# Batch numerators of a sketched attention: three batches as quads of 288 columns, and a new issue order

## Chip, cores and metric

One core of one Trainium2 chip. The metric is the device time of one execution in microseconds (us). A few hardware words: PE is TensorE (matmuls), DVE is VectorE, ACT is ScalarE, POOL is GpSimd, SP is SyncE, which here only issues DMAs. PSUM is the memory that PE writes; here it is eight banks of 512 float32 columns.

## The reference

An attention with degree-two sketch features, and then a mixing block over its output:

```python
def phi(x):                                   # 32 -> 64 features
    a = einsum('rd,bhsd->bhsr', S1, x)        # r = 8
    b = einsum('rd,bhsd->bhsr', S2, x)
    return einsum('bhsi,bhsj->bhsij', a, b).reshape(..., r * r)
q_p, k_p = phi(q), phi(k)
kv  = einsum('bhsf,bhsd->bhfd', k_p, v)
num = einsum('bhsf,bhfd->bhsd', q_p, kv)
den = einsum('bhsf,bhf->bhs', q_p, k_p.sum(2)) + 1e-06
x = (num / den) laid out as (B, S, H * D)

theta = x @ w_theta
zr, zi = x * cos(theta), x * sin(theta)
y = w_tok_r @ zr + w_tok_i @ zi               # over the 1088 tokens
u = x + y
out = u + relu(u @ w_ch)
```

There are 4 batches, 4 heads, 1088 tokens and a head dimension of 32, so x is 4 x 1088 x 128. The two token weights are 1088 x 1088.

## The kernel before

The tokens of a batch are 9 chunks of 128 (the last one holds 64). Three chunks make a group, so a batch has three groups of 384 columns. The kernel doesn't issue its work as it is written. Every step is first recorded by `op(engine, ..., function, writes, reads)`, each with a number; `vop` is the same for DVE. Then `run` takes the numbers in the order of a list written out by hand, `ORDER`, and `issue` calls the functions in that order. Each engine's own stream is the part of the list that belongs to it, executed in order; semaphores make a step wait for what it reads and for its buffers. A second list, `STARTS`, has a planned start for each step. `run` gives each buffer the slot of its class that has been free longest by these planned times, and `issue` puts short filler products (`spin`) on PE into planned gaps. Classes are sets of equal slots: `big` (22 of 1152 float32 columns), `zs` (5 of 2176), `g3` (5 of 768), `g1` (6 of 384), `ps` (the eight PSUM banks).

The stages of a batch are these.

- Keys: the features of k and their products with v (`kv`, 64 x 32 for each head). For batches 2 and 3, which are named in `QUADS`, kv is turned by two transposes and multiplied with a block mask into two halves of 32 features (`kvbd` of 256 columns). For 0 and 1 it is one transpose and 128 columns.
- Queries: `query_slices` turns q, and `levels` forms the two sketch factors in PSUM by products with q as weights (`exact`, `whole`). ACT copies them to `lv`, and a run of DVE steps ("den") scales one factor by the reciprocal of the denominator.
- Numerators, `outputs_x`. For each group DVE forms the outer products of the factors, 768 columns (`outer`). In batches 0 and 1 PE turns them (six transposes of 128 a group, line 1131), ACT copies them to SBUF (line 1135), two products on tiles of 128 x 64 give a group of x (`num`), and ACT copies that to `xT` (line 1144). In batches 2 and 3 DVE turns the features in 32 x 32 blocks (`V.transpose`, line 1109), and 32 products of 96 columns on the sixteen 32 x 32 tiles of PE (`quads`) give the group in four banks, which ACT copies by four copies of 96 columns (line 1121).
- Batches 1 to 3 (`XTURN`) also need x with tokens on the partitions. DVE turns the whole of `xT`, SP stores it to DRAM and fetches it back in another order.
- Angles: for each group, `theta` is a product on PE, ACT and DVE reduce the angle, ACT takes the two sines (lines 1203 and 1205), and DVE multiplies x with them into `z`.
- Token weights: 17 rows of 1088 KB come as 64-bit words, each into a `zs` slot. ACT (lines 643 and 645) and DVE decode a row into a `big` slot, in halves.
- Mixing: batches 0 and 1 are multiplied row by row (`mix_row`; "mix0_0" is all three groups of batch 0, 17 rows). Batches 2 and 3 are taken together by seven products of a Strassen-Winograd scheme (`winograd`), with additions on DVE and POOL.
- Outputs: `finish` multiplies with w_ch, adds on DVE, turns the result in 32 x 32 blocks and stores it. The last part of batch 3's first half (160 columns) goes by `finish_turned`, which transposes on PE instead.

Step 3 of the list is a dummy Sin of one column on ACT (line 433), issued before ACT's other work. Step 1 is 39 fillers on PE at the start.

Of the kernel before, what the change touches and what calls it, by code (L numbers as in the profile page):

```python
# [22 lines left out]
P = 128  # L23
# [115 lines left out]
)  # L139
WARM = 0  # L140
FILL = 5.0
LOAD_LEAD = 60.0
RAW_LEAD = 30.0
CHAINS = ((0,), (1,), (2, 3))
# [35 lines left out]
class Layout:  # L180
# [67 lines left out]
    def run(self):  # L248
        slots = {c: [[0.0, None] for _ in range(n)] for c, (n, _) in self.classes.items()}
        for b in self.bufs:  # L250
            b.left = len(b.ops)
# [52 lines left out]
def act(n):  # L304
    return 0.17 + 0.00083 * n
# [1238 lines left out]
```

## Time and profile before

| what | value |
|---|---|
| runs, us | 217.79, 218.53, 217.53 (median 217.79) |
| span of the profiled execution, us | 215.9 |
| median of the runs less that span, us | 1.9 |
| granted TensorE clock | 0.995 |
| busy PE / DVE / ACT / POOL, us | 208.9 / 174.3 / 114.5 / 59.7 |
| HBM read / written, MB | 29.84 / 4.00 |

The profile has one execution. Its span runs from the first to the last instruction; 1.9 us is what the median of the runs has beyond it, and stands in for the launch around the span. A group's line gives the code line, the engine, the operation, what it writes and reads with partitions x elements, the count, the busy time and the mean duration in ns. Nearly all PE products have the line 399, that of a helper, so they are told apart by buffer names and shapes. In the timeline a row is the start, the length and what ran. Products on PE are pipelined, so the distance between starts is their cost, not the length of one.

### The profile page before, as it was taken

What the parts mean: (1) busy time and instruction counts of PE and PEld (TensorE: products, weight loads), DVE (VectorE), ACT (ScalarE), POOL (GpSimd) and SP (SyncE); (2) the same over time, 40 slices, a digit from 0 to 9 for tenths busy, and PEclk for the clock granted to TensorE, in tenths of its full rate; (3) what the DMA queues carried; (4) which work ended last, traced back from release to release, by engine and by line L of the source; (5) the groups of instructions that cost most, each with busy time, mean ns of one, the idle gap of its engine ahead of it and who ended that gap; (6) DMA issues with size and microseconds to landing.
All of it is one profiled execution on the core that took longest, in us unless ns stands there. A gap on an engine that the chain in (4) does not pass through costs nothing.

```text
span 215.9 us, 5832 instructions
## 1 busy us (share of the span) xinstructions
PE 208.9 (97%) x2396; PEld 152.8 (71%) x2396; DVE 174.3 (81%) x343; ACT 114.5 (53%) x256; POOL 59.7 (28%) x105
## 2 busy tenths in 40 slices
PE   7899999999999999999999999999999999999992
PEld 7677798868866666866668666667677776666781
DVE  1799998999999998999999798885994747456263
ACT  4899989999998895798704233363810000000000
POOL 1272740306400000604004100000006489950403
PEclk9999999999999999999999999999999999999998
DMA  6999999995998993192002402424050420010735
GB/s 222 395 418 419 384 365 420 425 315 97 360 285 267 416 432 145 75 308 45 0 0 32 74 3 112 114 109 112 2 88 15 67 39 0 0 23 8 125 55 103
DMA packets 28046, 37.09 MB, mean 172 GB/s; under 512 B 20564, under 2 KB 23044, under 8 KB 25844
## 3 DMA queue, kind: packets, MB, share of 16 engines
q1 hardware_dynamic: 22868, 31.86, 42.4%
q0 software_dynamic: 1552, 3.25, 7.2%
q10 hardware_dynamic: 3600, 1.62, 2.8%
q8 instruction: 19, 0.31, 0.6%
q14 instruction: 7, 0.06, 0.1%
HBM read 29.84 MB, written 4.00 MB: 157 GB/s over the span
## 4 chain that ended last, share of the span: by engine, by line
PE 63%; DMA 18%; ACT 14%; issue 2%; SPq 1%; DVE 1%; POOL 1%; POOLq 0%; ACTq 0%
PE ps L399 61%; DMA zs<-w_tok 13%; DMA big<-k_l 5%; ACT big L645 4%; ACT big L643 3%; ACT lv L1056 1%; PE ps L1131 1%; ACT big L1021 1%; ACT g L1199 1%; ACT g L1202 1%; ACT g L1205 1%; ACT g L1203 1%; POOL out L1299 1%; SPq L671 0%; ACT g L1135 0%
## 5 line engine op out<-in xcount | busy, mean ns | idle before, releaser
L399 PE MATMUL ps<-big,zs 128*128 128x384 f32 (+2 forms) x380 | 110.5, 436 | 0.0
L399 PEld LDWEIGHTS ps<-big,zs 128*128 128x128 f32 x380 | 66.9, 190 | 32.5
L379 POOL TENSOR_TENSOR big<-big,big 128x544 f32<-128x544 f32 x16 | 22.1, 1458 | 48.6 <-DVE big L379 44.6
L399 PE MATMUL ps<-big,big 128*32 128x32 f32 (+2 forms) x352 | 22.8, 234 | 0.0
L643 ACT ACTIVATE big<-zs 128x1088 f32<-128x1088 f32 x17 | 20.9, 1231 | 1.5 <-DMA zs<-w_tok 0.9
L379 DVE CUSTOM_DVE_ANT_0 big<-big,big 128x2176 uint16<-128x2176 uint16 x17 | 21.5, 1275 | 0.0
L645 ACT ACTIVATE big<-zs 128x1088 int32<-128x1088 uint32 (+1 forms) x18 | 21.4, 1194 | 0.3 <-DMA zs<-w_tok 0.3
L1338 ACT COPY big<-ps 80x256 f32<-80x256 f32 x1 | 0.4, 368 | 39.6 <-DMA out<-g 39.6
L399 PEld LDWEIGHTS ps<-big,big 128*32 128x32 f32 (+1 forms) x352 | 15.3, 124 | 6.8 <-issue 0.8
L1276 ACT COPY g<-ps 128x384 f32<-128x384 f32 (+1 forms) x6 | 2.5, 466 | 23.4 <-PE ps L399 23.4
L379 DVE TENSOR_TENSOR big<-big 128x544 f32<-128x544 f32 x8 | 9.5, 1204 | 5.6 <-PE ps L399 5.6
L383 DVE TENSOR_SCALAR big<-big 128x1088 int32<-128x1088 int32 x17 | 12.2, 719 | 0.0
L379 POOL TENSOR_TENSOR mf<-mv,sm 128x32 f32<-128x32 f16 (+1 forms) x3 | 0.8, 262 | 39.1 <-DVE sm L379 39.1
L428 PE MATMUL ps<-idle 128*128 128x112 bf16 (+1 forms) x67 | 10.0, 312 | 1.3 <-POOL idle L430 1.3
L379 DVE TENSOR_TENSOR g<-lv 128x768 f32<-128x768 f32 x12 | 11.1, 950 | 0.1
L399 PEld LDWEIGHTS ps<-w,big 128*128 128x128 f32 (+1 forms) x76 | 9.8, 189 | 1.4
L379 DVE TENSOR_TENSOR big<-big,hf 128x1152 f32<-128x1152 f32 x8 | 10.7, 1351 | 0.0
L399 PE MATMUL ps<-w,big 128*128 128x128 f32 (+1 forms) x76 | 10.5, 278 | 0.0
L399 PE MATMUL ps<-sbk,g 128*128 128x64 f32 x72 | 10.0, 276 | 0.3 <-ACT g L793 0.3
L379 DVE TENSOR_TENSOR zs<-zs,g 128x384 f32<-128x384 f32 (+2 forms) x24 | 9.8, 447 | 0.2
L386 DVE SCALAR_TENSOR_TENSOR big<-ps,even,big 128x384 f32<-128x384 f32 (+1 forms) x10 | 4.8, 493 | 6.3 <-PE ps L399 6.2
L1199 ACT ACTIVATE g<-ps 128x384 f32<-128x384 f32 x12 | 5.9, 504 | 7.3 <-PE ps L399 7.3
(199 smaller groups left out, 379.2 us busy)
## 6 DMA issues: line engine op xcount, KB each, us to landing
zs<-w_tok SPq DMA_DIRECT2D x17, 1088.0 KB, 10.6
big<-k_l SPq DMA_DIRECT2D x5, 576.0 KB, 13.2
big<-v_l SPq DMA_DIRECT2D x4, 576.0 KB, 15.6
big<-q_l SPq DMA_DIRECT2D x3, 576.0 KB, 10.7
big<-hf POOLq DMA_DIRECT2D x3, 576.0 KB, 10.0
far<-zs SPq DMA_DIRECT2D x3, 576.0 KB, 2.8
zs<-far SPq DMA_DIRECT2D x12, 144.0 KB, 4.3
big<-k_l ACTq DMA_DIRECT2D x2, 576.0 KB, 4.4
```

The costliest lines, as they stand in the source:

```text
L379: eng.tensor_tensor(out=o, in0=a, in1=b, op=f)
L383: (eng or V).tensor_scalar(out=o, in0=a, scalar1=s1, scalar2=s2, op0=op0, **kw)
L386: (eng or V).scalar_tensor_tensor(out=o, in0=a, scalar=s, in1=b, op0=op0, op1=op1)
L399: T.matmul(o, lhs, rhs, start=start, stop=stop, skip_group_check=True)
L428: T.matmul(nowhere()[:, :n], idle()[:, 0:P], idle()[:, :n], start=True, stop=True, skip_group_check=True)
L643: op("A", 0.22 + n * 0.0009, lambda: A.activation(dfn(), words_of(raw(), n)[1].bitcast(F32), AF.Prelu, scale=2.0**-112, alpha=-(2.0**32)), ...
L645: op("A", 0.22 + n * 0.0009, lambda: A.activation(stp(), words_of(raw(), n)[0].bitcast(U32), AF.Copy, scale=2.0**-29), [stp], [raw])
L1021: op("A", act(GW) + 0.1, lambda g=g, tr=tr: A.activation(f()[:, g * GW:(g + 1) * GW], tr(), AF.Copy, scale=s()[:, 0:1]), [(f, g)], [tr, (s ...
L1056: op("A", act(480), lambda g=g, lp=lp: A.copy(lv().rearrange("p l (c n) -> p l c n", n=HR)[:, :, g * GC:(g + 1) * GC], lp().rearrange("p c ...
L1131: T.transpose(tr()[:, i * P:(i + 1) * P], qp()[:, i * H + 2 * n:i * H + 2 * n + 2].rearrange("p h i j -> p (h i j)"), ident())
L1199: op("A", act(GW), lambda cs=cs, th=th: A.activation(cs()[:, 0], th(), AF.Copy, bias=ROUND), [(cs, 0)], [th])
L1276: op("A", act(w), lambda: A.copy(u(), yp()[:, :w]), [uT], [yp])
```

## The change

- `QUADS` holds batch 1 too: its features are turned by DVE, its kv is prepared in two halves, and the transposes on PE and their copies are gone for it.
- In batches 1, 2 and 3 the three groups of turned features go to one buffer of 2304 columns, and there are 32 products of 288 columns for the whole batch in place of 32 of 96 for each group; four ACT copies of 288 columns follow. The buffer is of class `zs`, whose slots grow from 2176 to 2304 columns; `g3` has 4 slots for 5.
- In `levels`, `whole` takes only the 64 valid columns of the last chunk as weights.
- `finish_turned` is four recorded steps (transposes, copy, products, addition) with a buffer of its own for the result.
- The order is another one throughout. `STARTS` is gone: the slots are listed (`SLOTS`), and the fillers too (`GAPS`; 25 in all). Of the order itself: the dummy Sin comes behind the decoding of most rows; steps of batch 1's denominator come ahead of batch 0's first z, its outer products ahead of the last; SP issues rows 9 to 16 behind batch 1's way through DRAM; batch 3's last turn of 384 columns (step 908, with its stores) is the list's last step.

```diff
--- before
+++ after
 ORDER = (
-    29, 32, 4, 2, 5, 0, 1, 3, 34, 30, 356, 50, 33, 102, 44, 96, 6, 108, 103, 36, 7, 51, 366, 54, 144, 8, 97, 10, 9,
...
-    982, 925, 1000, 984, 983, 1008, 1001, 936, 1009, 1002, 1003, 937, 1004, 1005, 1010, 1006, 932, 1012, 1011, 933,
-    1013, 1007, 934, 938, 1014, 935, 1015, 939, 1016, 1017, 1018, 940, 1019, 941, 942, 943,
+    0, 4, 32, 1, 5, 29, 2, 33, 30, 144, 44, 139, 120, 108, 121, 143, 145, 6, 7, 109, 50, 146, 10, 140, 141, 126, 8, 9,
...
+    893, 894, 901, 902, 903, 986, 987, 818, 904, 980, 981, 989, 982, 954, 990, 895, 906, 905, 907, 909, 988, 955, 819,
+    983, 910, 911, 912, 913, 984, 914, 908,
 )
-STARTS = (
...
+GAPS = {51: 5, 11: 1, 79: 3, 90: 3, 92: 4, 436: 2, 168: 1, 117: 3, 119: 3}
+SLOTS = (
...
 WARM = 0
-FILL = 5.0
 LOAD_LEAD = 60.0
 RAW_LEAD = 30.0
 CHAINS = ((0,), (1,), (2, 3))
@@ -146,7 +98,7 @@
 KEEP = (2, 3)
 KEEP_CLS = "big"
 PAIR = (2, 3)
-QUADS = (2, 3)
+QUADS = (1, 2, 3)
 QTURN = (3,)
 XTURN = (1, 2, 3)
 PARTS = ((0, 384), (384, 544))
@@ -155,7 +107,7 @@
 RDMA = (False,) * 4
 QDMA = (False, False, False, False)
 UDMA = (True, True, False, False)
-TILE16, TILE32, TILE64, QUAD = 0.045, 0.12, 0.15, 0.65
+TILE16, TILE32, TILE64, QUAD = 0.045, 0.12, 0.15, 1.25
 ADD_FLY = 9.0
 ADD_FLY2 = 3.1
 QFIX = 2.006
@@ -246,33 +198,14 @@
         return o
 
     def run(self):
-        slots = {c: [[0.0, None] for _ in range(n)] for c, (n, _) in self.classes.items()}
-        for b in self.bufs:
-            b.left = len(b.ops)
         self.order = [self.ops[i] for i in ORDER]
-        for o, at in zip(self.order, STARTS):
-            o.start = at / 100.0
-            o.end = o.start + o.dur + o.fly
-            for b in o.bufs:
-                if b.slot is None and b.cls is not None:
-                    free = [(s[0], i) for i, s in enumerate(slots[b.cls]) if s[1] is None]
-                    b.slot = min(free)[1]
-                    slots[b.cls][b.slot][1] = b
-            for b in o.bufs:
-                b.left -= 1
-                b.end = max(b.end, o.end)
-                if not b.left and b.slot is not None:
-                    slots[b.cls][b.slot] = [b.end, None]
-
-    def issue(self, pools, fill, span):
-
-        last, on = 0.0, False
+        for b, slot in zip([b for b in self.bufs if b.cls is not None], SLOTS):
+            b.slot = slot
+
+    def issue(self, pools, fill):
         for o in self.order:
-            if o.eng == "P":
-                if on:
-                    for _ in range(int((o.start - last - 0.08) * FILL)):
-                        fill()
-                last, on = o.end, on and o is not span[1] or o is span[0]
+            for _ in range(GAPS.get(o.i, 0)):
+                fill()
             for b in o.bufs:
                 if b.ap is None:
                     b.ap = view(pools[b.cls](b.slot), b.shape, b.dt)
@@ -343,10 +276,10 @@
 
     classes = {
         "big": (22, 1152),
-        "zs": (5, 2176),
+        "zs": (5, 2304),
         "lv": (1, 5 * NT),
         "hf": (6, 576),
-        "g3": (5, 768),
+        "g3": (4, 768),
         "g1": (6, 384),
         "sm": (13, 192),
         "ps": (8, 512),
@@ -428,7 +361,7 @@
         T.matmul(nowhere()[:, :n], idle()[:, 0:P], idle()[:, :n], start=True, stop=True, skip_group_check=True)
 
     op("G", 0.3, lambda: G.memset(idle(), 0.0), [idle], [], due=-20.0)
-    first = op("P", 3.2, lambda: [spin(112) for _ in range(39)], [nowhere], [idle], due=-10.0)
+    op("P", 3.2, lambda: [spin(112) for _ in range(39)], [nowhere], [idle], due=-10.0)
     op("V", 1.25, constants, [hm, bdm, halfpi, ones], [])
     op("A", 1.5, lambda: A.activation(warm(), halfpi(), AF.Sin), [warm], [halfpi], due=0.0)
 
@@ -1048,8 +981,10 @@
 
             def whole(g=g, o=o):
                 for i in range(GC):
-                    x = f()[:, (g * GC + i) * P:(g * GC + i + 1) * P]
-                    mm(o(i)[:, 2 * HR:], x, mf[b]().rearrange("p t h r -> p (t h r)"), False, i == GC - 1)
+                    c = g * GC + i
+                    n = min(P, S - c * P)
+                    x = f()[:, c * P:c * P + n]
+                    mm(o(i)[:n, 2 * HR:], x, mf[b]().rearrange("p t h r -> p (t h r)"), False, i == GC - 1)
 
             op("P", 0.4, exact, [lp], [h, mv[b]], hold=[lv])
             op("P", 0.7, whole, [lp], [f, mf[b]])
@@ -1089,6 +1024,7 @@
         xt = xT[b] = buf("big", (NC * P,), F32, "xT")
         z = zt[b] = buf("zs", (NK, DM), F32, "z")
         bd = kvb[b]
+        qt = buf("zs", (NC, H, 2, SQ), F32, "qt") if b in QUADS else None
         for g in range(NG):
             at("num", b, "_", g)
             qp = buf("g3", (CH, R, R), F32, "qp")
@@ -1104,23 +1040,9 @@
             else:
                 vop(CH * R * R, lambda f=outer: f(V, 0, 1), [qp], [lv], lk=1)
             if b in QUADS:
-                qt = buf("g3", (GC, H, 2, SQ), F32, "qt")
-                xq = [buf("ps", (GC, SQ), F32, "xq") for _ in range(NQ)]
-                vop(CH * R * R, lambda qt=qt, qp=qp: V.transpose(out=qt().rearrange("p c h f t -> p (c h f t)"),
-                                                                 in_=qp().rearrange("p n i j -> p (n i j)")), [qt], [qp])
-
-                def quads(qt=qt, xq=xq):
-                    for f in range(2):
-                        for j in range(NQ):
-                            for h in range(H):
-                                u = slice(j * SQ, (j + 1) * SQ)
-                                mm(xq[j]()[h * D:(h + 1) * D], bd()[u, f, h], qt()[u, :, h, f], f == 0, f == 1)
-
-                op("P", QUAD, quads, xq, [bd, qt], hold=[xt])
-                for j in range(NQ):
-                    op("A", act(GC * SQ), lambda g=g, j=j, xq=xq: A.copy(
-                        xt().rearrange("p (c j t) -> p c j t", j=NQ, t=SQ)[:, g * GC:(g + 1) * GC, j], xq[j]()),
-                       cells(xt, g * GW, (g + 1) * GW), [xq[j]])
+                vop(CH * R * R, lambda g=g, qp=qp: V.transpose(
+                    out=qt()[:, g * GC:(g + 1) * GC].rearrange("p c h f t -> p (c h f t)"),
+                    in_=qp().rearrange("p n i j -> p (n i j)")), [(qt, g)], [qp])
                 continue
             qT = buf("g3", (2, GW), F32, "qT")
             for n in range(2):
@@ -1143,6 +1065,21 @@
             op("P", 0.8, num, [xp], [bd, qT], hold=[xt])
             op("A", act(GW), lambda g=g, xp=xp: A.copy(xt()[:, g * GW:(g + 1) * GW], xp()),
                cells(xt, g * GW, (g + 1) * GW), [xp])
+        if b in QUADS:
+            at("num", b)
+            xq = [buf("ps", (NC, SQ), F32, "xq") for _ in range(NQ)]
+
+            def quads():
+                for f in range(2):
+                    for j in range(NQ):
+                        for h in range(H):
+                            u = slice(j * SQ, (j + 1) * SQ)
+                            mm(xq[j]()[h * D:(h + 1) * D], bd()[u, f, h], qt()[u, :, h, f], f == 0, f == 1)
+
+            op("P", QUAD, quads, xq, [bd, qt], hold=[xt])
+            for j in range(NQ):
+                op("A", act(NC * SQ), lambda j=j: A.copy(
+                    xt().rearrange("p (c j t) -> p c j t", j=NQ, t=SQ)[:, :, j], xq[j]()), [(xt, ("q", j)) if j < NQ - 1 else xt], [xq[j]])
         src = xt
         if b == PAIR[1]:
             src = balance()
@@ -1329,25 +1266,27 @@
     def finish_turned(b, t0, w, u, keys, due):
         po, pu = (buf("ps", (GW,), F32, x) for x in ("po", "pu"))
         n = w // 2
-        y = lambda: xT[b]()[:n, 0:2 * DM]
+        yb = buf("g1", (2 * DM,), F32, "yb")
+        y = lambda: yb()[:n]
+
+        def turned():
+            for c in range(2):
+                T.transpose(pu()[:n, c * DM:(c + 1) * DM], u()[:, c * n:(c + 1) * n], ident())
 
         def products():
-            parts = [u()[:, c * n:(c + 1) * n] for c in range(2)]
-            for c, uc in enumerate(parts):
-                T.transpose(pu()[:n, c * DM:(c + 1) * DM], uc, ident())
-            A.copy(y(), pu()[:n, 0:2 * DM])
-            for c, uc in enumerate(parts):
-                mm(po()[:n, c * DM:(c + 1) * DM], uc, w2()[:, 1], True, True)
-
-        op("P", w * 4 / 2400 + 0.01, products, [po, pu], keys + [w2])
-        vop(w, lambda: stt(y(), po()[:n, 0:2 * DM], 0.0, y(), ALU.max, ALU.add), keys, [po])
-        vop(w, lambda: None, [], keys)
+            for c in range(2):
+                mm(po()[:n, c * DM:(c + 1) * DM], u()[:, c * n:(c + 1) * n], w2()[:, 1], True, True)
+
+        op("P", 0.2, turned, [pu], keys, hold=[yb])
+        op("A", act(2 * DM), lambda: A.copy(y(), pu()[:n, 0:2 * DM]), [yb], [pu])
+        op("P", 0.35, products, [po], keys + [w2])
+        vop(2 * DM, lambda: stt(y(), po()[:n, 0:2 * DM], 0.0, y(), ALU.max, ALU.add), [yb], [po])
 
         def store(E, c):
             E.dma_start(out[b, t0 + c * n:t0 + (c + 1) * n, :], y()[:, c * DM:(c + 1) * DM])
 
-        op("S", w * P * 2 / 100e3, lambda: store(SY, 0), [], keys, due, lk=2)
-        op("A", 0.92, lambda: store(A, 1), [], keys, due, fly=2.1)
+        op("S", w * P * 2 / 100e3, lambda: store(SY, 0), [], [yb], due, lk=2)
+        op("A", 0.92, lambda: store(A, 1), [], [yb], due, fly=2.1)
 
     def winograd(t):
         p, q = PAIR
@@ -1467,7 +1406,7 @@
                 kfeatures(b)
         chain_out(bs)
         if not bs[0]:
-            last = op("P", 0.1, spin, [nowhere], [kvb[WARM]] if WARM < B else [idle])
+            op("P", 0.1, spin, [nowhere], [kvb[WARM]] if WARM < B else [idle])
     for b in range(B):
         query_slices(b)
     for i in range(NK):
@@ -1497,7 +1436,7 @@
                 mix_out(b, g, yp, t + 6.0 + (3.0 * g[0] if b == 0 else 0.0))
     L.run()
     with tc.manual_schedule():
-        L.issue(pools, spin, (first, last))
+        L.issue(pools, spin)
 
 
 # ---- launch: one core; numpy lays the arrays out, in their own types ----
```

150 rows, old and new, of tables (ORDER, SLOTS, STARTS) are left out of this document.

## The prediction

> **What bounds the kernel now.** I read the table of engines first, then busy time by stretch, the chain that ended last, and the groups by shape; the issue order in the code says which row belongs to which step.
>
> ```profile
> PE 208.9 (97%) x2396; PEld 152.8 (71%) x2396; DVE 174.3 (81%) x343; ACT 114.5 (53%) x256; POOL 59.7 (28%) x105
> ```
>
> TensorE (PE) is busy 97% of 215.9 us. The stretches (PE, PEld, DVE, ACT, POOL, clock, DMA share, GB/s) show that it is not alone:
>
> ```profile
> 50.00:60.00 10.00, 10.00 (x258) 8.26 (x255) 9.96 (x15) 9.93 (x20) 6.04 (x12) 1.00 0.77 242
> 60.00:70.00 10.00, 10.00 (x143) 6.67 (x142) 10.00 (x15) 9.34 (x15) 0.00 (x0) 1.00 0.93 269
> ...
> 90.00:100.00 10.00, 10.00 (x55) 7.25 (x55) 9.93 (x15) 9.74 (x16) 0.67 (x4) 1.00 0.75 229
> 100.00:110.00 10.00, 10.00 (x36) 6.35 (x35) 9.90 (x21) 5.67 (x8) 1.73 (x2) 1.00 0.00 0
> ```
>
> From 50 to 110 us PE and VectorE (DVE) are both full; after 140 only PE is. The clock is 1.00. The chain's end (start, us, engine):
>
> ```profile
> 77.02 1.27 ACT big L645
> 78.42 3.41 PE ps L399 x55
> ...
> 123.58 86.46 PE ps L399 x601
> 210.38 0.50 DVE g L1303
> 211.17 0.46 POOL out L1299
> 211.77 0.62 POOL out L1299
> ```
>
> From 78.42 it is PE, then 3.7 us of tail behind the last product (212.17). PE has in fact no gap from 57.16, where the first product of batch 0's mixing (`mix0_0`) starts, to 212.17: 155.0 us. So PE work removed there is worth its length, if DVE can follow.
>
> **PE, the numerators.** The groups, and the timeline around one old group of 32 products:
>
> ```profile
> L399 PE MATMUL ps<-g,g 32*32 32x96 f32 x384 | 5.8, 252 | 0.0
> L1131 PE MATMUL ps<-ident,g 128*128 128x128 f32 x36 | 5.3, 278 | 0.2 <-DVE g L379 0.2
> L399 PE MATMUL ps<-g,sm 128*64 128x384 f32 x24 | 5.0, 507 | 0.0
> ```
>
> ```profile
> 119.09 0.96 PE L399 MATMUL ps<-g,g 32*32 32x96 f32 x64
> 119.98 1.24 PE L399 MATMUL ps<-big,zs 128*128 128x384 f32 x3
> ```
>
> A float32 product is two instructions, so 384 are six groups of 64. A group holds PE from 119.09 to 119.98, 0.89 us, and the product behind it takes 0.11 longer than its usual 0.645: 1.00 each, 6.0 in all. Batch 1's way, from the timeline: transposes 0.75+0.71+0.67 at 76.01, 81.76 and 83.08, products 0.80+1.45 at 80.96 and 85.89: 4.4. Removed: 10.4.
>
> Added: three groups of 288 columns. A pass of 384 columns is spaced 0.3225 us, so one of 96 takes 0.08; 64 instructions over 16 tiles are four passes per tile, 0.32 of the 0.89; 0.57 is fixed. With 288 columns: 0.97+0.57 = 1.54, plus 0.11: 1.65, 4.95 for three. Bounds: 0.97 if the fixed part disappears beneath longer passes, 2.67 if all grows in proportion; I take the split, since 0.57 over 64 instructions is 9 ns each, which looks like issue. Batch 1's preparation of kv gains one pair of transposes for a single one (0.26 for 0.17): 0.1. PE saves 10.4-5.05 = 5.35; 7.1 and 2.0 at the ends.
>
> The Trainium skill ("TensorE: Matmul & The Clock Gate", Part 3, packing) measures 10.6 times for 16 tiles; 64 passes of 0.24 us would by that be an estimated 1.45 us a group, 0.3 us less over three. No run here shows that shape.
>
> **ACT and DVE.** ACT loses six copies of L1135 (0.499), three of L1144 (0.492) and 24 of 96 columns (0.252), 10.5 us, and gets 12 of 288 columns: between 0.252 and 0.49, say 0.40, 4.8. It saves 5.7, worth nothing by itself: PE or DVE is last. DVE gains three turns:
>
> ```profile
> L1109 DVE STREAM_TRANSPOSE g<-g 128x768 f32<-128x768 f32 x6 | 5.9, 976 | 0.7 <-PE ps L399 0.6
> ```
>
> 2.9 us, in the stretch where DVE is full, and 0.1 for a wider kv step. A quad (the 32 products) now waits for all three turns of its batch; behind it on PE stand the mixing rows.
>
> **The other order.** I summed the rows' durations along the two lists, each cut at the next start on its engine. Before, batch 0's z (which releases `mix0_0`) ends with 50.4 us of DVE work done, at 56.63: DVE idled 6.2, mostly in the first 10 us. In the new order 51.8 us stand up to it, because steps of batch 1's denominator come earlier. With the same idle time z ends at 58.0 and `mix0_0` starts at 58.6, 1.4 later; 155.0-5.4 = 149.6 of PE work follows: 208.2. The same sum at other joints: DVE work up to the third turn of batch 1 is 60.7, plus 6.3, plus 141.5 of PE from its quad on: 208.6, the latest; batch 2's level products (behind q's second half on DVE), its kv and batch 1's first mixing give 208.0 to 208.6. The same sum for before gives 212.1, against 212.17 seen. So PE ends 3.6 earlier at best, with six joints within 1 us; a late arrival at any adds directly. I put 0.5 for that (0 to 3).
>
> The dummy Sin that opens ACT's list (L433) moves behind the decodes. Its row:
>
> ```profile
> L433 ACT ACT_TABLE_LOAD x1 | 1.3, 1283 | 1.6 <-PEq L1534 1.6
> ```
>
> If a load of 1.28 lands before batch 0's first Sin instead, ACT can bear it: it has 47.3 us of work up to there against 48.5 before, while DVE has 1.4 more, so ACT leads by some 3 us. Without that cover it costs 1.3. The Trainium skill ("ScalarE: Activation LUTs", What ACT_TABLE_LOAD costs) gives 1283 ns, as the row, and 1380 for a drain, 2.66 per change of set; by it a second load would still fit the lead. No run here shows a second one.
>
> The 64-column last chunk shortens weights, not moving columns (96 as before): nothing; if loading bounds those products, under 0.1. Splitting the transposed last output of batch 3 lets its ACT copy run aside: PE work is the same.
>
> **The tail.** Before, the last POOL store was issued until 212.98 and the span ended 2.9 later. In the new list DVE's last operation is batch 3's 384-column turn (0.57), after the last product's addition (0.42), and POOL issues two stores behind it (0.46 and 0.62). PE's end + 0.11+0.42+0.57, 0.3 to POOL, 1.2 of issue, 2.9: 5.5, against 3.7: 1.8 lost.
>
> Sum: 215.9-3.6+0.5+1.8 = 214.6 of span. The median of the runs is 217.79, 1.9 above the profiled span; the same 1.9 makes 216.5.
>
> **Rivals.**
> 1. *Everything is kept.* DVE idles less at the start, as its first 10 us hold only 3.93 of work, and the last stores overlap: PE ends at 208.2, tail 3.7, 211.9 of span: 213.8. For it: PE showed no stall at all before. Against: the tail's order is written down.
> 2. *Late raw rows; slower.* SP now issues rows 9 to 16 of the token weights behind batch 1's turn through DRAM (its store waits for a DVE turn, the fetch for the store); behind these waits on SP stand all later rows. The turn ends by the sum at 71.7 (65.4 of DVE work plus 6.3), the store takes 2.8, so row 9 is issued at 74.7. Before, rows 10 to 15 went out from 65.0 on, free of the turn. ACT is to decode row 9 at 79.5, and behind that decode come batch 1's last sines, which DVE needs at 84.9. With the mean landing of 10.6 (`zs<-w_tok`) row 9 is there at 85.3, the sines at 88.1: DVE and with it PE lose 3.2: 217.8 of span, 219.7. It decides from a landing of 7.4. Against: with little else in flight 1088 KB at the 420 GB/s of the table of slices need 2.7.
> 3. *The quads do not widen well:* 2.67 each, 3.4 more on PE: 218.0, time 219.9.
> 4. *DVE slows beside POOL.* One DVE addition of 128x544 took 4.59 us at 177.13 while POOL ran L379 back to back, against 0.72 for its kind; the new order again sets such runs beside each other, with about 3 us of slack: up to 1 us, so its time is the forecast's and it has no chance of its own.
>
> **How the numbers follow.** A measurement can tell 0.5%, 1.1 us, from no change: faster is below 216.7, slower above 218.9. Forecast (215.4 to 217.9) 0.47; rival 1 0.23; rival 2 0.20; rival 3 0.07; 0.03 for anything worse. Faster: rival 1 and two thirds of the forecast's case, 0.54. Slower: rivals 2 and 3 less their milder forms, 0.25. Same: 0.21. The range leaves out the best of rival 1 and the worst of the others: 213.0 to 220.0.
>
> **What would show it.** Right: three groups of 64 instructions 32x288 holding PE some 1.5 us each; no L1131 for batch 1; nine turns at L1109; `mix0_0` at 58 to 59 and PE dense behind it; PE's end near 209; POOL's last stores 2 us behind it. Wrong: idle time on PE between 58 and 110, released by DVE or ACT (rival 2, if ACT waits for `zs<-w_tok`); quads of over 2 us; an ACT table load beside batch 0's Sin that PE waits for; `mix0_0` at 57 or earlier.

## The result and the profile after

The changed kernel takes 241.12 us (median of 4, 239.83 to 241.30) against 217.66 for the kernel before (217.45 to 218.53): a ratio of 1.104, 95% interval 1.099 to 1.108. It is slower, and far outside the range forecast. The profiled execution has a span of 239.4 us against 215.9; the forecast was 214.6.

The page of after: the table of engines, and the granted clock in 40 slices of 6.0 us.

```profile
PE 219.6 (92%) x2173; PEld 156.1 (65%) x2173; DVE 185.0 (77%) x346; ACT 113.8 (48%) x236; POOL 63.6 (27%) x104
...
PEclk9996579999995999999999999999999995999999
```

PE has 223 products fewer and yet is busy 10.7 us longer than before (208.9), and idle for 19.8 instead of 7.0. The digits 6, 5, 7 at the start, 5 in the middle and 5 near the end are stretches at half clock: by the clock's records 19.8 to 33.4, 70.9 to 77.8 and 197.2 to 204.1. Before, the mean was 0.995.

The stretches of after (PE, PEld, DVE, ACT, POOL, clock, DMA share, GB/s):

```profile
10.00:20.00 10.00, 6.94 (x251) 5.75 (x250) 6.85 (x18) 5.73 (x18) 6.08 (x21) 0.99 1.03 389
20.00:30.00 10.00, 8.26 (x109) 6.71 (x107) 4.57 (x14) 5.26 (x19) 3.60 (x11) 0.50 1.04 394
...
60.00:70.00 10.00, 8.13 (x90) 6.50 (x90) 8.85 (x17) 8.52 (x23) 6.34 (x10) 1.00 0.81 222
```

The first two rows are the heart of it. For the same two stretches the trace of before answers:

```profile
10.00:20.00 10.00, 9.74 (x204) 7.88 (x203) 9.62 (x20) 9.87 (x26) 4.86 (x17) 1.00 1.02 417
20.00:30.00 10.00, 9.97 (x198) 7.91 (x197) 9.62 (x27) 9.30 (x27) 4.64 (x12) 1.00 1.02 373
```

Before, PE, DVE and ACT are full from 10 us on. After, DVE does 11.4 us of work in these 20 where it did 19.2, with the transfers equally full. DVE's work up to `mix0_0` comes later, and from 60 to 70, where PE was full before, it waits (8.13).

The end of the chain of waits of after (start, us, engine, work), answering to the one shown of before:

```profile
190.75 0.78 DVE zs L312
...
195.60 1.85 DVE big L312
...
200.77 32.51 PE ps L332 x132
...
235.28 0.61 POOL out L1236
```

In place of 86 us of PE without a break, the chain runs through DVE's late additions. The groups and the timeline of after show what the change itself was to bring (L332 is the helper that was L399, L1043 the turn that was L1109):

```profile
L1043 DVE STREAM_TRANSPOSE zs<-g 128x768 f32<-128x768 f32 x9 | 8.5, 960 | 0.1
```

```profile
83.56 1.60 PE L332 MATMUL ps<-zs,g 32*32 32x288 f32 x64
85.09 0.88 PE L332 MATMUL ps<-sm,pbd 128*128 128x128 f32 x6
```

A quad holds PE from 83.56 to 85.09, 1.53 us; 1.54 was forecast.

Against the forecast, PE's end is the place to settle accounts. It was to come at 209.1 (212.17 - 3.6 + 0.5) and comes at 233.96, 24.9 later. `mix0_0` starts at 73.50 instead of 58.6: 14.9. From there PE takes 160.5 instead of 150.5: 10.0, of which 5.0 are waits, and 4.8 are half of some 9.6 us that PE ran at half clock (70.9 to 77.8 from 73.5 on, and 197.2 to 204.1 less a wait of 1.62). The tail is 5.4, as forecast (5.5).

### The profile page after: what moved, and what is told of

The parts are those of the page before. It is cut to its first block, busy times and chain, and to the rows that moved or that the text cites. A ratio compares the mean times of both kernels' runs of the same rounds, so it can differ in the third digit from the quotient of the medians.

```text
span 239.4 us, 5359 instructions
## 1 busy us (share of the span) xinstructions
PE 219.6 (92%) x2173; PEld 156.1 (65%) x2173; DVE 185.0 (77%) x346; ACT 113.8 (48%) x236; POOL 63.6 (27%) x104
## 3 DMA queue, kind: packets, MB, share of 16 engines
q10 hardware_dynamic: 3600, 1.62, 2.5%
## 4 chain that ended last, share of the span: by engine, by line
PE 62%; DMA 12%; DVE 9%; ACT 8%; issue 5%; SPq 1%; POOL 0%; POOLq 0%; DVEq 0%
PE ps L332 57%; DMA zs<-w_tok 8%; DVE big L312 4%; DMA big<-k_l 3%; PE ps L361 2%; ACT big L576 2%; PE ps L951 2%; DVE g L312 1%; DVE zs L312 1%; PE ps L723 1%; ACT big L578 1%; DMA far<-zs 1%; DVE big L316 1%; SPq L1102 1%; ACT g L1142 1%
## 5 line engine op out<-in xcount | busy, mean ns | idle before, releaser
L332 PE MATMUL ps<-big,zs 128*128 128x384 f32 (+2 forms) x380 | 112.7, 445 | 1.8 <-DVE zs L312 1.6
L332 PEld LDWEIGHTS ps<-big,zs 128*128 128x128 f32 x380 | 67.8, 194 | 38.3 <-issue 3.1
L332 PE MATMUL ps<-big,big 128*32 128x32 f32 (+2 forms) x352 | 24.5, 241 | 3.8 <-DVE big L312 3.2
L312 POOL TENSOR_TENSOR big<-big,big 128x544 f32<-128x544 f32 x16 | 22.9, 1461 | 10.4 <-DVE big L312 8.6
L332 PEld LDWEIGHTS ps<-big,big 128*32 128x32 f32 (+1 forms) x352 | 15.4, 126 | 12.4 <-DVE big L312 4.1
L326 POOL DMA_DIRECT2D g<-big x6 | 5.3, 964 | 55.4 <-ACT g L1213 55.4
L319 DVE SCALAR_TENSOR_TENSOR big<-ps,even,big 128x160 f32<-128x160 f32 (+1 forms) x10 | 4.9, 497 | 13.7 <-PE ps L332 13.7
L312 DVE TENSOR_TENSOR zs<-zs,g 128x384 f32<-128x384 f32 (+2 forms) x24 | 11.5, 519 | 2.2 <-DMA out<-g 1.1
L332 PE MATMUL ps<-sbk,g 128*128 128x64 f32 x72 | 11.5, 304 | 1.7 <-issue 1.7
L361 PE MATMUL ps<-idle 128*128 128x112 bf16 (+1 forms) x65 | 10.7, 331 | 1.3 <-POOL idle L363 1.3
L332 PE MATMUL ps<-w,big 128*128 128x128 f32 (+1 forms) x76 | 10.9, 282 | 0.6 <-ACT big L1066 0.6
L332 PEld LDWEIGHTS ps<-w,big 128*128 128x128 f32 (+1 forms) x76 | 9.7, 189 | 2.5 <-ACT big L1066 1.2
L1236 POOL DMA_DIRECT2D out<-g x8 | 5.0, 636 | 22.0 <-DVE g L1240 22.0
L312 DVE TENSOR_TENSOR big<-big,hf 128x1152 f32<-128x1152 f32 x8 | 10.7, 1352 | 0.0
L332 PEld LDWEIGHTS ps<-sbk,g 128*128 128x128 f32 x72 | 10.2, 215 | 0.5
```

The source lines that it names most:

```text
L312: eng.tensor_tensor(out=o, in0=a, in1=b, op=f)
L319: (eng or V).scalar_tensor_tensor(out=o, in0=a, scalar=s, in1=b, op0=op0, op1=op1)
L326: op("G", 0.9, lambda: G.dma_start(dst(), src(), accum_op=ALU.add), w, r, fly=fly)
L332: T.matmul(o, lhs, rhs, start=start, stop=stop, skip_group_check=True)
L361: T.matmul(nowhere()[:, :n], idle()[:, 0:P], idle()[:, :n], start=True, stop=True, skip_group_check=True)
L1236: E.dma_start(out[b, s0:s0 + n, f * SQ:(f + 1) * SQ].rearrange("(c j) i -> j c i", j=SQ), ot()[f * SQ:(f + 1) * SQ, :n].rearrange("j (c i) ...
```

## The experiments

Three places lose the time: the first 40 us, the start of `mix0_0`, and 190 to 205. The theories were that PE's halts and half clock at the start do it (the order put its small products too close together), that the second table load or late token rows do it, and that POOL holds up DVE late; against these stood that the numerators themselves (wide quads, three more turns) cost it, in any order. A run without an interval is a single execution; the kernel before took 217.6 to 218.2 beside them.

### The dummy Sin at the front again: `sin_first`

```diff
 ORDER = (
-    0, 4, 32, 1, 5, 29, 2, 33, 30,
...
-    317, 318, 508, 509, 678, 406, 348, 349, 400, 408, 407, 426, 3, 409, 416,
+    0, 4, 32, 1, 5, 29, 2, 3, 33, 30,
...
+    317, 318, 508, 509, 678, 406, 348, 349, 400, 408, 407, 426, 409, 416,
```

> The changed kernel with the dummy Sin back at the front of ACT's list. Its profile has a second ACT_TABLE_LOAD of 1.28 us at 66.7, in the chain that ended last, and the clock is halved in the three stretches 19.7-33.4, 70.9-77.8 and 197.2-204.0 us. If the load matters by its own length only: one load left, mix0_0 1.3 earlier, span 238. If the PE idle time around it (64 to 71 us) is also what brings the second half-clock stretch: that stretch goes too, and the span falls by 1.3+3.4, to some 234.7. If the 3 us lead of ACT that the prediction counted on hides it: no change, 239.4.

In after the groups show a first load at L626, and ACT's timeline a second:

```profile
L626 ACT ACT_TABLE_LOAD x1 | 1.3, 1283 | 1.6 <-PEq L1473 1.6
```

```profile
66.66 1.28 ACT L1142 ACT_TABLE_LOAD   x1
67.96 0.52 ACT L1142 ACTIVATE g<-g 128x384 f32<-128x384 f32 x1
```

The run took 240.46 us, span 238.7. The second load is gone, but `mix0_0` starts at 73.85 and the clock is halved from 17.0 to 40.9. So this run does not price the load: it came with a half-clock stretch 10.2 us longer than that of after. `thin_all` below comes back to it.

### Fillers into the early gaps: `fill`

```diff
-GAPS = {51: 5, 11: 1, 79: 3, 90: 3, 92: 4, 436: 2, 168: 1, 117: 3, 119: 3}
+GAPS = {51: 5, 11: 1, 79: 3, 90: 3, 92: 4, 436: 2, 168: 1, 117: 3, 119: 3, 62: 6, 67: 6, 69: 6, 71: 6, 73: 6, 75: 4, 104: 4}
```

> The changed kernel with 36 more filler products in PE's list, ahead of steps 62 to 104 (13.5 to 19 us), nothing else. PE stops at 15.4 for 2.35 us and at 22.4 for 1.74 in the middle of a step, at instructions 449 and 705 of its list, 256 apart, and each time an instruction fetch of 16 KB is under way (15.4-16.5, 21.8-22.8). Theory A: PE runs small products faster than their instructions come (256 in 2.9 us; the kernel before takes 5.4 to 6.8 for each 256 there), the idle time halves the clock from 19.7 to 33.4, and that is the main loss. Then fillers, which take 0.16 us for two instructions, remove both stops and the first half-clock stretch, and mix0_0 (73.5 now) starts at 64 to 68; the span falls to 228 to 234. Theory B: the early part is late because DVE and ACT are late in the new order, and PE only waits: 36 fillers of 0.16 us then change nothing, or add up to 5.8: 239 to 245.

The edit adds 38 fillers (36 by the count in the expectation). 244.2 us, span 242.4, `mix0_0` at 76.34. From 8 us up to the half clock PE has no gap above 0.4 us, and the clock is halved all the same, only later (27.5 to 41.1):

```profile
PEclk9999756999999999999999999999999996899997
```

The number expected is missed. Fillers make PE's list longer and give nothing back, and gaps that the profile shows are not the only thing that halves this clock.

### The late sums on DVE: `ac3_dve`

```diff
-APOOL = ("4", "3")
+APOOL = ("4",)
```

> The changed kernel with the eight additions of 544 columns for the seventh product (asum 3) on DVE in place of POOL. In the profile one DVE addition of 256 columns takes 5.01 us at 190.67 (0.42 for its kind) while POOL runs six additions back to back, PE waits 3.03 and 1.62 us for DVE, and the clock is halved from 197.2 to 204.0. Theory A, DVE is held up by POOL: the long addition and PE's waits go, the half-clock stretch with them, and the span falls by 4.7+3.4, to some 231; DVE's 5.7 us of added work find room, as DVE is 76% busy there. Theory B, DVE is simply behind with its own work there: the 5.7 us are added to it, and the span is 239 to 245.

235.63 us, span 233.9: 5.5 less. Eight additions of 128x544 move from POOL to DVE. In after, DVE's and POOL's timelines and the two late waits of PE are:

```profile
190.67 5.01 DVE L312 TENSOR_TENSOR zs<-zs 128x256 f32<-128x256 f32 x1
```

```profile
191.45 8.52 POOL L312 TENSOR_TENSOR big<-big,big 128x544 f32<-128x544 f32 x6
```

```profile
197.50 1.65 PE L332 MATMUL ps<-big,big 128*128 128x384 f32 x2 [3.03 <-DVE big L312]
200.77 0.90 PE L332 MATMUL ps<-big,zs 128*128 128x160 f32 x2 [1.62 <-DVE zs L312]
```

In `ac3_dve` the same addition and the same two waits read:

```profile
192.45 0.41 DVE L312 TENSOR_TENSOR zs<-zs 128x256 f32<-128x256 f32 x1
```

```profile
193.55 0.91 PE L332 MATMUL ps<-big,big 128*128 128x384 f32 x2 [1.25 <-DVE big L312]
195.17 0.78 PE L332 MATMUL ps<-big,zs 128*128 128x160 f32 x2 [0.71 <-DVE zs L312]
```

An addition of 0.41 us takes 5.01 beside POOL's run. With the run gone the waits are 1.96 instead of 4.65, and the late half-clock stretch is 3.4 us instead of 6.9. Not all of the 5.5 is due to this: PE comes to the first of the two waits at 192.30, in after at 194.47, though `mix0_0` starts at 73.76 here: this run has no half clock from 73.5 to 77.8. So 2.2 us lie ahead of the waits, and some 3.3 belong to the edit. The Trainium skill ("SBUF — State Buffer", Who interferes with whom) says that VectorE and GpSimd share one pair of ports under an exclusive lock. The 5.01 against 0.41 agrees; the trace can't separate a wait for a lock from a slower operation.

### The three together: `all3`

> The three edits together (dummy Sin first, 36 fillers, asum 3 on DVE). If the three half-clock stretches and the idle time ahead of them are the whole loss: mix0_0 at 59 to 63, PE dense behind it, span 215 to 221. If the causes lie elsewhere, as much as the sum of the single ones shows.

239.1 us, span 237.3: worse than `ac3_dve` alone. The clock is full until 38.3, then halved for 13.7 us behind a stop of PE of 1.98 (see `thin_rest`); `mix0_0` starts at 77.08. The late waits are 1.25 and 0.71 again. It says once more that fillers don't mend the start.

### The old order up to mix0_0: `early_old` and `early_old_ac3`

`early_old` is the changed kernel with the list of the kernel before, and its fillers, up to `mix0_0` on each engine, and the new list behind it; the slots are given out anew for that (`g3` has 5 again, `sm` 11 for 13).

```diff
 ORDER = (
-    0, 4, 32, 1, 5, 29, 2, 33, 30, 144, 44, 139, 120, 108, 121, 143, 145, 6, 7, 109, 50, 146, 10, 140, 141, 126, 8, 9,
...
+    29, 32, 4, 2, 5, 0, 1, 3, 34, 30, 356, 50, 33, 102, 44, 96, 6, 108, 103, 36, 7, 51, 366, 54, 144, 8, 97, 10, 9, 11,
...
```

> The changed kernel, but each engine takes the steps up to mix0_0 in the order, and with the fillers, of the kernel before; behind that the new order goes on with what is left (slots listed anew, g3 with 5 slots). The fillers of the run before this one did not bring mix0_0 forward (76.3): they took the place of the stops, so they could not tell a slow supply of instructions from late inputs. If the early order is the cause of the first 15 us: mix0_0 at 57 to 58, clock at 1.00 until then, and with DVE work of the same length behind it PE ends at 212 by the sums, plus 5 of waits beside POOL and 3.4 of half clock, plus 5.4 of tail: span 222 to 227. If the quads or batch 1's new way are the cause, mix0_0 stays beyond 65.

238.63 us, span 236.8. `mix0_0` starts at 57.34 with the clock at 1.00 until then: 16.2 earlier than after, and as before (57.16). So the order of the start with its fillers and slots, and nothing of the numerators, costs the first 15 us. The total hardly moves, because the joint of the two lists then costs what was won. The timeline of PE:

```profile
57.34 2.10 PE L332 MATMUL ps<-big,zs 128*128 128x384 f32 x6
65.44 1.45 PE L332 MATMUL ps<-big,big 128*32 128x32 f32 x72 [6.00 <-DMA big<-hf]
```

PE stands for 6.00 us in sums of batch 1 and the clock is halved from 64.7 to 78.4. That wait comes from the splice, not from the change.

> The same with asum 3 on DVE in place of POOL. In the run that had this edit alone the waits of 3.03 and 1.62 us became 1.26 and 0.71, the half-clock stretch 3.4 instead of 6.9, the span 5.5 less. If the early order and this are independent: 5 less than early_old, 216 to 221.

The same with the late sums on DVE (`APOOL = ("4",)`): 235.08 us, span 233.3, 3.5 less; the late waits are 1.24 and 0.70. With the 3.3 above, that is the second run in which this edit is worth 3 to 4 us.

### The wide quads alone in the old order: `old_quads`, `old_quads_late`

The kernel before, its order and fillers, with batches 1, 2 and 3 as wide quads with three DVE turns each:

```diff
-QUADS = (2, 3)
+QUADS = (1, 2, 3)
```

(It is the changed kernel in all but its order, fillers and slots, so the 64-column last chunk and the split last output are in it too; a batch's quad stands where the last of its three groups stood.)

> The quads of 288 columns for batches 1, 2 and 3, turned by DVE, in the order of the kernel before: each kept step at its old place, batch 1's turns right behind its outer products, a quad where the last product of its batch stood (six steps moved by up to 12 places for free slots). If the prediction's step on PE is right (5.35 us saved) and DVE does not bind: span 211, 5 less than before. If DVE binds, by its sum of work ahead of batch 3's quad plus 6.2 idle plus PE's work behind it: PE ends at 213.1, span 216.8, no gain. If the clock falls somewhere, more.

223.31 us, span 221.5: 5.7 slower than before, although `mix0_0` starts at 57.33. PE's timeline names the waits:

```profile
78.09 0.88 PE L332 MATMUL ps<-g,big 128*32 128x64 f32 x48 [0.91 <-DVE g L312]
84.75 1.51 PE L332 MATMUL ps<-sm,pbd 128*128 128x128 f32 x6 [3.24 <-DVE sm L312]
...
139.71 1.59 PE L332 MATMUL ps<-zs,g 32*32 32x288 f32 x64 [2.65 <-DVE zs L1043]
```

PE is busy 207.3 us, about 2.9 of them because 83.7 to 90.5 ran at half clock (5.7 us behind the wait that ended at 84.75, halved): 204.4, 4.5 below the 208.9 of before. The saving forecast (5.35) is thus real by some four fifths, and eaten by 7 us of waits for DVE. The three turns of batch 1 (2.9 us) sit in the stretch where DVE is full, and what comes late is a step behind them, in the denominators of batches 2 and 3 (`sm,pbd`).

> old_quads with batch 1's three turns moved on DVE behind the steps of the key chain of batches 2 and 3 and of batch 2's queries (13 us later), and its quad two rows of mix0_0 further on PE. In old_quads the turns held up that chain: PE waited 0.91 and 3.24 us, and the clock was halved from 83.7 to 90.5. If that was the cause: no wait and no half clock there, and the span is 221.5 less 4.2 and 3.4, to 214. If DVE's 3 us simply come out later (DVE is full until 110): waits of 2 to 3 us at batch 2's levels or at batch 3's quad, 216 to 219.

Here batch 1's turns stand some 13 us later on DVE, and its quad two mixing rows later on PE. 223.36 us, the same. The 0.91 and 3.24 are replaced by 1.21, 0.39, 1.31, 1.20 and 1.03 between 80 and 100 us: 5.1 in all; the 2.65 at batch 3's quad stays. In neither of the two places were DVE's added 3 us hidden.

### The kernel before without fillers: `before_nofill`

```diff
-FILL = 5.0
+FILL = 0.0
```

> The kernel before without the 27 fillers between 11 and 36 us (FILL 5.0 to 0.0; the 39 at the start stay). If idle time on PE halves the clock there: a half-clock stretch between 17 and 41 us, mix0_0 3 to 10 us later than 57.2, span 219 to 226. If the clock holds: 57 and 216.

232.09 us against 217.62, span 230.2: dropping 27 filler products, which take PE some 0.16 us each, makes the kernel 14.5 us slower. The clock row of its page:

```profile
PEclk9955555899999997699999999999999999999999
```

It is halved from 10.9 to 41.6, and `mix0_0` starts at 66.35 instead of 57.16: 9.2. The other 5 us come behind that, with a stop of 2.23 us at 87.9 (see `thin_rest`) and half clock from 89.4 to 96.2. The fillers planned into gaps by `STARTS` hold the clock at the start; the change has 25 and puts them at other places. `fill` shows that more of them is no cure by itself.

### Fewer instructions in the same time: `thin_rest`

```diff
                 def two(c=c):
+                    if c:
+                        spin()
+                        return
```

It leaves out batch 0's remainder sums over chunks 1 to 8 and runs one filler for each chunk: 120 products and 120 weight loads fewer, PE's time about the same.

> The changed kernel with batch 0's remainder products (steps 68 to 75, 16 instructions of 32 columns each with their weight loads) left out for chunks 1 to 8, one filler of 384 columns in the place of each: the same time on PE (0.16 us for 0.15 to 0.24), 240 fewer instructions of the 256 that a fetch brings. It leaves out part of k's remainder in batch 0's kv scale. If PE stops at 15.4 and 22.4 because its instructions come too late: both stops go, the half-clock stretch from 19.7 goes or shortens, and mix0_0 comes 4 to 11 us earlier than 73.5. If PE waits there for something else (a slot, a DMA): stops of the same length stay.

232.78 us, span 231.0, `mix0_0` at 67.28: 6.2 earlier than after, with no early half clock. What it removes is seen in PE's timeline of after:

```profile
15.14 0.23 PE L332 MATMUL ps<-big 128*32 128x32 f32 x5
17.72 0.19 PE L332 MATMUL ps<-big 128*32 128x32 f32 x1 [2.35 <-issue]
...
24.14 0.27 PE L332 MATMUL ps<-sbk,g 128*128 128x64 f32 x1 [1.74 <-issue]
```

PE stops in the middle of a step, for 2.35 and 1.74 us, with nothing in the profile that it waits for ("issue"). Both stops lie at PE's records 449 and 705, 256 apart; each time the queue of instruction transfers (q8) brings 16 KB, 256 instructions of 64 bytes, between 15.4 and 16.5 and between 21.8 and 22.8. The 256 instructions ahead of the first stop took PE 2.9 us, those ahead of the second 4.7; in the kernel before the first five such stretches take 5.7 to 7.0, and each transfer ends 2.2 us or more before PE needs it. So PE outran its instructions while transfers were full (DMA share 1.03).

Counted by the records in the traces of all the runs here, before and after among them, PE begins no block of 256 sooner than 1.2 us after the end of its transfer, and wherever it stops for more than 0.1 us on the border of two blocks it goes on 1.2 to 1.5 us after that end. Two stops of other runs are of this kind, in the timelines of `all3` and `before_nofill`:

```profile
38.31 2.93 PE L332 MATMUL ps<-mf,big 128*128 128x96 f32 x12 [1.98 <-DVE big L316]
```

```profile
90.13 0.24 PE L399 MATMUL ps<-sq,sm 32*32 32x16 f32 x3 [2.23 <-issue]
```

PE goes on there at records 1218 and 2754, three and nine blocks behind 450, 1.4 us after the transfer's end. In `all3` the profile names a DVE step, but that had ended at 37.90, and the weight load beside the product shows "issue".

With 240 instructions fewer PE no longer stops there for more than 0.13 us; its first gap of note is a load of data, by the timeline of `thin_rest`:

```profile
26.15 0.54 PE L332 MATMUL ps<-g,big 128*32 128x64 f32 x24 [1.82 <-DMA big<-v_l]
```

The Trainium skill ("Runtime: NRT & Kernel Launch", Instruction fetch mechanics) gives the same 16 KiB blocks of 256 instructions, and calls the crossing mostly hidden. The blocks agree; the two stops do not. The 6.2 us are the stops and the half clock together, and no run separates them: `fill` has neither stop, but 38 more fillers and as long a half clock.

### All that was found, on the new order: `thin_all`

`thin_rest` (with what it leaves out), the Sin first, and the late sums on DVE.

> thin_rest (part of batch 0's remainder sums left out, fillers in their place) with the dummy Sin first and asum 3 on DVE. In thin_rest mix0_0 began at 67.3 with the clock at 1.00 throughout the early part, an ACT table load of 1.28 us at 61.5 ahead of batch 0's sines, and waits of 3.04 and 1.62 us beside POOL at 186 with 6.9 us of half clock behind them. If these are separate losses: mix0_0 at 66.0, no half clock, span 231.0-1.3-2.7-3.4, 223 to 225. What is then left against the forecast of 214.6 is the 7 to 8 us by which mix0_0 is late for other reasons (late data for PE, ACT and SP in the new order of loads).

227.68 us, span 225.9, the clock at 1.00 to the end; slower than expected. `mix0_0` starts at 66.19, 1.1 before that of `thin_rest`: this is about the 1.28 of the load that ACT no longer carries. The late waits are 1.26 and 0.71.

It is still 10 us above the kernel before, and 9.0 of them stand ahead of `mix0_0` (57.16 before); against the 58.6 forecast it is 7.6. PE waits for loads of v (1.82) and others. In after the chain of waits lies on PE from 11.60 to 53.04 almost without a break, the two stops among it; in `thin_all` it leaves PE at 20.42 and runs through a row of token weights:

```profile
22.51 19.96 DMA zs<-w_tok
```

ACT decodes that row at 42.55, having waited 1.02 for it. So with PE's stops gone the late data come to the fore. The new order asks for them in another sequence while the transfers are full; no run here tests that sequence, so this part stays open.

### Batches 2 and 3 alone: `quads23`, `quads23b`, `quads23c`

The kernel before with only those two quads widened, since batch 1 costs DVE time it doesn't have. (The 64-column last chunk, the split last output and slots listed anew are in these three runs too.) A batch's turns and quad stand where those of its last group stood.

> The order and fillers of the kernel before, batch 1 as before, and only the quads of batches 2 and 3 widened: one of 288 columns in the place of the third of 96 (five steps moved by up to 12 places). DVE has nothing added. By the prediction's sum, with the 1.3 us that a wide quad took in the profiles of the changed kernel: six times 1.00 less two times 1.5 is 3.0 us saved on PE, from 119 us on, where PE alone is full: span 213, time 214.7, ratio 0.986. If waiting for all three turned groups costs it (PE waited 2.65 us for batch 3's third turn in old_quads, where DVE ran 6 us late): 215 to 216 of span, no change.

219.58 us against 217.98, ratio 1.007 (1.004 to 1.010). Its two quads save 2.7 on PE (6.0 less 2 x 1.64), but PE waits 2.65 at batch 3's, in its timeline and DVE's:

```profile
134.21 1.59 PE L332 MATMUL ps<-zs,g 32*32 32x288 f32 x64 [2.65 <-DVE zs L1043]
```

```profile
130.85 1.36 DVE L1097 STREAM_TRANSPOSE zs<-big 128x1152 f32<-128x1152 f32 x1
...
133.08 0.98 DVE L1043 STREAM_TRANSPOSE zs<-g 128x768 f32<-128x768 f32 x1
```

A narrow quad could start on its own turn. The wide one waits for the third, which stands behind batch 2's whole turn (1.36). The clock is halved for 3.4 us after that wait; the runs spread with it, from 217.85 at a mean clock of 0.998 to 220.72 at 0.984.

`quads23b` puts the third group's outer products and turn ahead of batch 2's turn, and the quad two products later (steps by their numbers in the list: 747, 748, 749 are batch 3's outer products and turn, 750 to 754 its quad and copies):

```diff
-    610, 657, 696, 697, 698, 745, 699, 710, 711, 632, 611, 747, 712, 658, 700, 703, 748, 701, 612, 749, 704, 659, 713,
-    705, 840, 838, 755, 750, 702, 633, 706, 751, 526, 752, 753, 754, 762, 634, 756, 635, 769, 757, 613, 758, 660, 614,
+    610, 657, 696, 697, 698, 745, 699, 710, 711, 632, 611, 747, 748, 749, 712, 658, 700, 703, 701, 612, 704, 659, 713,
+    705, 840, 838, 755, 702, 633, 706, 526, 750, 751, 752, 753, 754, 762, 634, 756, 635, 769, 757, 613, 758, 660, 614,
```

> quads23 with two places changed. In quads23 a wide quad holds PE for 1.53 us (124.09 to 125.62) as forecast, but batch 3's waits 2.65 us for the third turned group, whose outer product and turn stand on DVE behind batch 2's angle step and its 1.36 us turn, and the clock is halved from 136.1 to 139.5. Here these two DVE steps come ahead of them (1.9 us earlier), and the quad comes two products later on PE (1.3 us). If that wait and its half clock are all that ate the 3 us: no gap at 131, clock 1.00, span 217.7-2.65-1.7 = 213.4, time 215.2, ratio 0.988. If the wide quad itself brings no gain: 217 to 218.

219.4 us against 217.93, ratio 1.005 (1.002 to 1.008). The 2.65 has become two waits, of 1.03 and 0.78, and still a half-clock stretch of 3.5 us.

`quads23c` also lets batch 2's angle step (`theta2_0`) go ahead of that turn on DVE, the quad one product later still, and two products between it and batch 3's first angles:

```diff
+    610, 657, 696, 697, 698, 745, 699, 710, 711, 632, 611, 747, 748, 749, 712, 658, 703, 612, 704, 659, 713, 705, 700,
+    701, 840, 838, 755, 702, 633, 706, 526, 634, 750, 751, 752, 753, 754, 756, 635, 757, 613, 762, 758, 660, 769, 614,
```

> quads23b with two more places changed. There the quad of batch 3 stopped in its middle for 1.03 us (two of its four PSUM slots still held angles that DVE had not read, behind a 1.36 us turn), and the next product waited 0.78 for the last of the four copies; the clock was halved for 3.4 us. Here DVE's reading of the second angle comes ahead of the turn, the quad comes one product later, and two products stand between it and the angles that need its copies. If short waits and the half clock behind them are all that is left: no gap, clock 1.00, span 217.6-1.8-1.75 = 214.0, time 215.9, ratio 0.991. If DVE or the copies are simply late: waits of the same sum elsewhere, 217 to 218.

216.88 us against 218.13, ratio 0.994 (0.993 to 0.996). One wait of 1.21 is left (at 144.2), which halves no clock:

```profile
PEclk9999999999999999999999999999999999999999
```

It beats both kernels, the one before by 0.6%: 1.25 us of the 2.7 that the two quads take off PE. A ratio of 0.991 was expected.

## Why the prediction was wrong

- **The numerators on PE: right.** 1.53 us a quad for 1.54, nine turns at 0.960 for 0.976, no transposes for batch 1. In the old order PE's work falls by 4.5 for 5.35. ACT's copies of 288 columns take 0.41 for 0.40.
- **The order, "with the same idle time z ends at 58.0 and `mix0_0` starts at 58.6": the step that failed.** It summed durations along two lists and carried 6.2 us of DVE idle time and a full clock over from a trace with another list. `mix0_0` came at 73.50. DVE idles 10.6 us more between 10 and 50 us. `early_old` puts 16 us of `mix0_0`'s start down to the order; `thin_rest` puts 6.2 of them down to PE running out of instructions and the half clock behind it, `thin_all` 1.1 to the table load, and 7 to 8 stay open. Neither an instruction transfer nor fillers had a term, although the diff removed `STARTS` and `FILL`; in the old order `before_nofill` prices the fillers at 9.2 up to `mix0_0` and 14.5 in all.
- **The added turns: mis-sized.** I placed 2.9 us on DVE "in the stretch where DVE is full" and let them hide behind slack of under 1 us at six joints, for 0.5. In `old_quads` they come out as 7 us of waits, and `old_quads_late` moves them without hiding them. That a quad waits for all three turns was named and left without a price: 2.65 us at one batch (`quads23`).
- **DVE beside POOL: right in kind, wrong in size.** "Up to 1 us" was 2.7 of waits (4.65 for 1.96 without POOL's run) and 3.5 us more at half clock, 1.7; the edit is worth 3.3 in `ac3_dve` and 3.5 in `early_old_ac3`, each a single run. The row that warned of it (4.59 us at 177.13) was already quoted; I took the slack of the sum as its price in place of that row.
- **The table load: the cover was gone.** ACT was to lead by 3 us. The load stands at 66.66, right between the angle's last step on ACT and the sine, with ACT busy on both sides, and costs about its own 1.28 (1.1 in `thin_all`).
- **The tail: right**, 5.4 for 5.5.
- **The rivals.** Late raw rows would have stopped PE for 3.2 us between 80 and 90: from 73.5 to 190 no wait of PE is above 0.21. (The 10.6 us of landing used there is the page's median, not a mean.) The quads did widen. No rival had the clock or PE's instructions in it.

## What to carry to other kernels

When a change brings a new issue order, durations of the old trace don't add up to the new start: count what each engine issues in a stretch, see whether the fillers that hold the clock are still in it, and expect idle time to change. Work taken off a full engine and put on another full engine gains nothing until its place on the second one is found; widening a product that needs three inputs also makes it wait for the last. Change one of these at a time: two quads with their order retuned are worth 0.6%, while the whole of the change lost 10%.

## What the runs showed of the hardware

- The clock came at 1.00 or at half, in stretches of about 3.4 us or multiples (3.4, 6.8, 10.2, 13.7, 23.9, 30.7). The Trainium skill ("TensorE: Matmul & The Clock Gate", Part 1) gives two rates and a window of 3413 ns, and agrees. Its rule to avoid idle gaps above about 3.4 us does not suffice here: 2.35 us in after, 2.65 in `quads23`, and 1.03 and 0.78 within 3.2 us in `quads23b` each preceded a half-clock stretch, while a single 1.21 in `quads23c` did not. But the same 2.65 at batch 3's quad in `old_quads` was followed by full clock, and in `fill` the clock was halved at 27.5 with no gap above 0.4 between 8 us and there. So the length of a gap does not settle it here, and what does stays open.
- PE began no block of 256 instructions sooner than 1.2 us after the end of its 16 KB transfer. Up to record 2754, the six blocks of all runs that it ran in 2.9 to 4.8 us at a DMA share of 0.85 or more were each followed by a stop of 1.7 to 2.4 us; the 14 that it ran in 4.7 to 4.9 us at a share of 0.72 or less were followed by none.
- One DVE addition of 0.41 us took 5.01 beside a run of POOL additions.
